# Sums of a weight matrix's quarters: made twice, or made once, stored to DRAM and loaded

## The chip, the cores and the metric

The kernel runs on one core of a Trainium2 chip. The metric is the device time of one execution in microseconds (us). The kernel before took 429.52 us, the median of three runs (427.53 to 430.59).

## What is computed

The reference mixes two branches of the same input by a learned gate, for x of shape (1, 2048, 512), 32 heads of width 16 and a hidden width of 1376. In short form:

```python
g = sigmoid((x * gate_w).sum(-1, keepdims=True))

# branch a: linear attention with a two-sided softmax feature map
q, k, v = split_heads(x @ wqkv)                     # 32 heads, 16 wide
pq, pk  = q @ w_phi, k @ w_phi                      # per head 16 x 16
phi_q   = concat(softmax(pq), softmax(-pq))         # 32 wide; phi_k likewise
kv, z   = phi_k^T v, sum_s phi_k
o       = (phi_q kv) / (phi_q z + 1e-6)
a       = merge_heads(o) @ wo

# branch b: dense, Mish, dense
b = mish(x @ w1 + b1) @ w2                          # w1: 512 x 1376

out = g * a + (1 - g) * b
```

All is fp32. The factor on w_phi's drawn values is 200.

## The kernel before

**Precision.** Every matrix product is made of fp32r pieces: an operand is split into a high part (an fp32r copy, made on ScalarE) and a low part (operand minus high part, subtracted on GpSimd or VectorE), and three products are added in PSUM: high by high, high by low, low by high.

**Stages.** Eight chunks "A0" to "A7" run over the sequence and build the key side: kv and z. Then four blocks "B0" to "B3" of 512 rows make the query side, the second dense layer ("down"), the output projection ("wo") and the mix. The first dense layer ("up", w1 by x) is made in two superblocks, "S0" for the blocks 0 and 1 and "S1" for the blocks 2 and 3.

**Pairs.** Ten of the eleven column tiles of w1 are taken as five pairs per superblock. A pair's part of w1 is a 2 x 2 matrix of quarters, and so is the superblock's x; the four results are made of seven quarter products instead of eight (a scheme of Strassen and Winograd), which needs sums of w1's quarters and of x's quarters. `pair_ops(p)` defines the steps of a pair. For pair 0 in S1 they are called `S1.wr_0` and so on:

- `wr`: load the quarters into the tile w1r, on SP's queue.
- `wa`, `wb`: split the quarters that enter the products unsummed, into w1d and w1o (high parts on ScalarE, low parts on GpSimd).
- `ws` (function `su`, L687 to L690): four VectorE instructions that make the sums in place in w1r.
- `wc` (function `hi2`): one ScalarE copy, the high part of all the sums, into w1sh.
- `wd` (function `lo2`, L700): one GpSimd subtraction, the low part, into w1sl.
- `p1` to `p7`: the seven products on TensorE; `p5`, `p6`, `p3` and `p7` use w1sh and w1sl.
- `c1`, `c5`, `c6` (copies out of PSUM on ScalarE), `a2`, `a3`, `a7` (additions on VectorE, L740, L743, L746), `mA0` to `mB1` (Mish on ScalarE), `sB0`, `sB1` (stores of block 1's or 3's results "ab" to DRAM, L762).

The quarters of w1 are the same in both superblocks, and so are their sums; x's are not. In pair 0 of S1, w1sh and w1sl are the two halves of one tile w1e.

**Order.** A string, RUN, names every step of the program in the order in which it is to be issued. Each instruction is pinned, so every engine runs its own instructions in that order, and so does each DMA queue. Nearly all DMAs are issued from SyncE's queue ("SP"): a DMA that waits there, for a buffer or for its data, holds up those behind it. Buffers come from pools by tag: six tiles of 1024 columns "m4" (w1d, w1o, w1sh, w1sl, woh, wol among them), three of tag "tx" (w1r, raw, xr), and others.

**Around the pairs.** SP's queue carries, beside w1: the exponentials of a block's query side, transposed on VectorE (L969), stored as "ed" (L971) and read back as eight pieces "eT" (L992; the step `B2.mv0` reads eight); the query projections, stored as pqd and read back as "pq" (L950); the stored results "ab", read back as "actb" (L811); the key sums z, transposed on VectorE and sent as "zd" (L859) and read back, spread over the partitions, as "zb" (L863); VectorE multiplies E by zb at L954. The output projection's weights come as "raw" (L578).

Helper lines: every matmul is recorded at L118, every ScalarE activation at L138.

Of the kernel before, what the change touches and what calls it, by code (L numbers as in the profile page):

```python
# [8 lines left out]
F32 = mybir.dt.float32  # L9
# [5 lines left out]
P = 128  # L15
# [91 lines left out]
def tile_gated_mix(ctx: ExitStack, tc: tile.TileContext, xT, wv, wkT, wqT, bd, w1a, w1b, b1, w2a, w2b, wo, out):  # L107
# [6 lines left out]
    pin = tc.keep_in_program_order  # L114
    V, G_, A_, Sy = nc.vector, nc.gpsimd, nc.scalar, nc.sync
# [4 lines left out]
    def T(shape, dt, tag, bufs, name):  # L120
        nm[0] += 1
        return sp.tile(shape, dt, name=f"{name}_{nm[0]}", tag=tag, bufs=bufs)

    def k8(name, tag, dt=F32R):
        return T([P, 2048], dt, tag, {"x": 7, "eT": 2, "E": 2, "w2": 5}[tag], name)

    def k4(name, tag, dt=F32):
        return T([P, 1024], dt, tag, {"tx": 3, "m4": 6, "z": 1}[tag], name)
# [8 lines left out]
    def act(out_, in_, fn=AF.Copy, **k):  # L137
        return pin(A_.activation(out_, in_, fn, **k))  # L138

    def kt(t, f):  # L140
        return t[:, : KT * f].rearrange("p (k f) -> p k f", f=f)
# [4 lines left out]
    def f32(ap):  # L146
        return ap.bitcast(F32)
# [445 lines left out]
    def w1_dram(f):  # L593
        d, f, n = (w1a, f, NFA) if f < NFA else (w1b, f - NFA, NFB)
        return d.rearrange("p (k n f) -> p k n f", k=KT, n=n)[:, :, f : min(f + 2, n), :]

    def s_ops(q):
        key = ("S", q)
        bs = 2 * q, 2 * q + 1
# [49 lines left out]
        def pair_ops(p):  # L649
            fs = W2G[p]  # L650
            i0, i1 = 1 + 2 * p, 2 + 2 * p
            W, ps, v = {}, {}, {}
# [29 lines left out]
                pin(G_.tensor_sub(o[1], r[:, 2:, P:], f32(o[0])))  # L682

            def su():
                r = kt(W["r"], 256)
                a11, a21, a22, a12 = r[:, :2, :P], r[:, :2, P:], r[:, 2:, :P], r[:, 2:, P:]
                pin(V.tensor_add(a22, a22, a21))  # L687
                pin(V.tensor_add(a21, a21, a11))
                pin(V.scalar_tensor_tensor(a11, a11, -1.0, a22, op0=ALU.mult, op1=ALU.subtract))
                pin(V.tensor_sub(a12, a12, a11))  # L690

            def hi2():
                if q and not p:
                    W["8"] = k8("w1e", "eT")
                W["sh"] = W["8"][:, :1024] if "8" in W else k4("w1sh", "m4", F32R)
                act(W["sh"], W["r"])

            def lo2():
                W["sl"] = W["8"][:, 1024:] if "8" in W else k4("w1sl", "m4", F32R)
                pin(G_.tensor_sub(W["sl"], W["r"], f32(W["sh"])))  # L700

            def dv(k0):
                return [a[:, k0 : k0 + 2, :] for a in halves2(W["d"])]
# [61 lines left out]
            for name, fn in (("wr", ld), ("wa", hi1), ("wb", lo1), ("ws", su), ("wc", hi2), ("wd", lo2), ("p1", p1), ("p2", p2), ("p3", p3), ("p4", p4),  # L765
                             ("p5", p5), ("p6", p6), ("p7", p7), ("a2", a2), ("a3", a3), ("a7", a7),
                             ("c1", lambda: copy("A0", "a")), ("c6", lambda: copy("B0", "a")), ("c5", lambda: copy("B1", "b"))):
                at(key, f"{name}_{n}", fn)
# [5 lines left out]
        for p in range(NFB):  # L774
            pair_ops(p)

        for m in range(2):
            b, W = bs[m], {}
# [300 lines left out]
    for q in range(NB // 2):  # L1079
        wo_ops(q)  # L1080
        s_ops(q)
# [153 lines left out]
```

## Time and profile before

| | |
|---|---|
| median of three runs | 429.52 us (427.53 to 430.59) |
| the profiled execution | 432.84 us; span 431.1 us, mean granted clock 0.996 |
| TensorE busy (weight loads apart) | 422.3 us, 98% |
| VectorE | 369.3 us, 86% |
| GpSimd | 263.6 us, 61% |
| ScalarE | 253.6 us, 59% |
| DMA | 74.06 MB, mean 172 GB/s |

The profile records one execution. PE is TensorE's matmuls, PEld its weight loads, DVE VectorE, ACT ScalarE, POOL GpSimd; SPq is SyncE's DMA queue. Busy times are sums over the span. A row of a timeline gives start, length, engine, line, operation, output and input, and in brackets the idle time before it and what released it; a row of a group gives busy time, mean nanoseconds of one, and idle time before; a row of a DMA group gives the count, the size of one and the median us from issue to landing. The span runs from the first to the last record, and the time of the execution contains 1.7 us beside it.

### The profile page before, as it was taken

Reading aid. Unit: us, or ns where it says so; the run is one execution under the profiler, and the core shown is the slowest. Engines: PE = TensorE matmul, PEld = TensorE weight load, DVE = VectorE, ACT = ScalarE, POOL = GpSimd, SP = SyncE. Lnnn points to the kernel's source line nnn. Section 1 sums busy time; section 2 is a strip of 40 time slices with the busy share of each in tenths; the row PEclk is TensorE's granted clock in tenths of the full one; section 3 lists DMA queues with packets and bytes.
Section 4 is the critical chain, followed back from the end, with each engine's and each line's share of the span. In section 5 each row is a group of like instructions: output and inputs, shape, how many; then the busy total and the mean of one; then the engine's idle time right before and its main releaser. Section 6 shows DMA issues by size and latency. Waiting matters only on the chain. (4 is left out here: it accounts for less than half of the span.)

```text
span 431.1 us, 7558 instructions
## 1 busy us (share of the span) xinstructions
PE 422.3 (98%) x2772; PEld 340.2 (79%) x2772; DVE 369.3 (86%) x519; ACT 253.6 (59%) x373; POOL 263.6 (61%) x186
## 2 busy tenths in 40 slices
PE   8999999999998999899999999999999999999996
PEld 7888888888886877688878687788788887877875
DVE  3899789998998999998999998799989699999512
ACT  3574463646254899768679813467978467851131
POOL 2298868799674966635666494977455627541220
PEclk9999999999999999989999999999999999999999
DMA  7900597675988344433888477833533725555532
GB/s 260 366 34 28 164 273 182 140 179 126 209 171 214 108 134 123 160 109 122 235 249 281 165 239 237 281 91 122 177 119 143 232 73 188 179 199 168 197 121 75
DMA packets 52670, 74.06 MB, mean 172 GB/s; under 512 B 8085, under 2 KB 32149, under 8 KB 52633
## 3 DMA queue, kind: packets, MB, share of 16 engines
q1 hardware_dynamic: 50440, 66.36, 47.9%
q0 software_dynamic: 1904, 6.82, 9.5%
q8 instruction: 22, 0.36, 0.3%
q10 hardware_dynamic: 288, 0.39, 0.3%
q14 instruction: 16, 0.12, 0.1%
HBM read 43.53 MB, written 28.85 MB: 168 GB/s over the span
## 5 line engine op out<-in xcount | busy, mean ns | idle before, releaser
L118 PE MATMUL down<-w2g,h 128*128 128x512 f32 x316 | 98.5, 393 | 0.0
L118 PEld LDWEIGHTS down<-w2g,h 128*128 128x128 f32 x316 | 58.6, 188 | 14.8 <-issue 2.5
L118 PE MATMUL down<-w2g,l 128*128 128x512 f32 x158 | 61.8, 391 | 0.2 <-POOL l L824 0.2
L824 POOL TENSOR_TENSOR l<-act,h 128x512 fp32r<-128x512 f32 (+1 forms) x24 | 32.3, 1345 | 41.2 <-ACT h L138 16.7
L824 POOL TENSOR_TENSOR l<-actb,h 128x512 fp32r<-128x512 f32 x20 | 29.0, 1451 | 38.3 <-ACT h L138 20.7
L138 ACT ACTIVATE E<-E 128x1024 f32<-128x1024 f32 x32 | 33.4, 1057 | 16.5 <-DVE E L285 7.1
L118 PE MATMUL up<-x,w1sh 128*128 128x512 f32 x144 | 39.7, 397 | 2.2 <-DVE act L740 2.1
L118 PE MATMUL wo<-woh,ohl 128*128 128x512 f32 x128 | 40.9, 389 | 0.0
L118 PEld LDWEIGHTS down<-w2g,l 128*128 128x128 f32 x158 | 29.6, 188 | 7.5 <-POOL l L824 1.2
L118 PEld LDWEIGHTS up<-x,w1sh 128*128 128x128 f32 x144 | 26.7, 189 | 9.2 <-DVE act L740 2.5
L700 POOL TENSOR_TENSOR w1sl<-w1r,w1sh 128x1024 fp32r<-128x1024 f32 x9 | 22.2, 2467 | 18.0 <-ACT w1sh L138 17.4
L118 PE MATMUL proj<-tw,sx 128*128 128x512 f32 x126 | 31.5, 394 | 1.5 <-ACT qs L138 1.5
L628 POOL TENSOR_TENSOR x<-xr,x 128x1024 fp32r<-128x1024 f32 x10 | 26.7, 2666 | 3.6 <-ACT x L138 3.6
L118 PEld LDWEIGHTS proj<-tw,sx 128*128 128x128 f32 x126 | 23.3, 188 | 6.9 <-ACT qs L138 1.9
L138 ACT ACT_TABLE_LOAD x22 | 28.2, 1283 | 0.4
L118 PEld LDWEIGHTS wo<-woh,ohl 128*128 128x128 f32 x128 | 24.0, 188 | 5.0
L138 ACT ACTIVATE act<-act,b1s 128x512 f32<-128x512 f32 x30 | 21.4, 719 | 10.9 <-DVE act L740 4.1
L118 PE MATMUL up<-x,w1d 128*128 128x512 f32 x108 | 27.7, 398 | 0.0
L267 POOL TENSOR_TENSOR xl<-xraw,xh 128x512 fp32r<-128x512 f32 x14 | 18.3, 1370 | 15.3 <-ACT xh L138 15.0
L138 ACT ACTIVATE act<-up 128x512 f32<-128x512 f32 x30 | 17.6, 590 | 16.8 <-PE up L118 16.4
L138 ACT ACTIVATE h<-actb 128x512 fp32r<-128x512 f32 x20 | 12.4, 628 | 24.4 <-DMA actb<-ab 18.9
L118 PE MATMUL wo<-wol,ohl 128*128 128x512 f32 x64 | 24.9, 389 | 0.0
(173 smaller groups left out, 1086.4 us busy)
## 6 DMA issues: line engine op xcount, KB each, us to landing
ed<-E SPq DMA_DIRECT2D x16, 512.0 KB, 3.1
eT<-ed SPq DMA_DIRECT2D x64, 128.0 KB, 3.2
za<-E POOLq DMA_DIRECT2D x11, 512.0 KB, 6.8
xr<-in_xT_dram SPq DMA_DIRECT2D x20, 256.0 KB, 4.2
ab<-act SPq DMA_DIRECT2D x20, 256.0 KB, 2.9
actb<-ab SPq DMA_DIRECT2D x20, 256.0 KB, 3.3
pqd<-qs SPq DMA_DIRECT2D x16, 256.0 KB, 5.8
pq<-pqd SPq DMA_DIRECT2D x16, 256.0 KB, 3.6
```

The lines of the kernel that those rows point to most:

```text
L118: return pin(nc.tensor.matmul(*a, **k))
L138: return pin(A_.activation(out_, in_, fn, **k))
L267: pin(eng.tensor_sub(xs[c][1][j], kt(rawx[c], SC)[:, 2 * j : 2 * j + 2, :], f32(xs[c][0][j])))
L628: pin((V if n in LOV else G_).tensor_sub(X[n][:, 1024:], xr[n], f32(X[n][:, :1024])))
L700: pin(G_.tensor_sub(W["sl"], W["r"], f32(W["sh"])))
L824: pin(G_.tensor_sub(U[i]["l"][:n, :], U[i]["a"][:n, :], f32(U[i]["h"][:n, :])))
```

## The change

The first superblock still makes the sums, their high part and their low part, and now also stores both parts to DRAM tiles (`wsd[p]`, two of 512 KB for each pair). The second superblock no longer makes them: `su` returns at once, and `hi2` and `lo2` load the stored parts into the tiles that they filled before. The steps keep their places in RUN.

```diff
@@ -594,6 +594,8 @@
+    wsd = {}
+
     def s_ops(q):
...
             def su():
+                if q:
+                    return
                 r = kt(W["r"], 256)
                 a11, a21, a22, a12 = r[:, :2, :P], r[:, :2, P:], r[:, 2:, :P], r[:, 2:, P:]
                 pin(V.tensor_add(a22, a22, a21))
@@ -693,11 +697,20 @@
                 if q and not p:
                     W["8"] = k8("w1e", "eT")
                 W["sh"] = W["8"][:, :1024] if "8" in W else k4("w1sh", "m4", F32R)
+                if q:
+                    pin(Sy.dma_start(f32(W["sh"]), wsd[p][0]))
+                    return
                 act(W["sh"], W["r"])
+                wsd[p] = [tc.dram_tile([P, 1024], F32, name=f"ws{p}_{x}") for x in range(2)]
+                pin(Sy.dma_start(wsd[p][0], f32(W["sh"])))
 
             def lo2():
                 W["sl"] = W["8"][:, 1024:] if "8" in W else k4("w1sl", "m4", F32R)
+                if q:
+                    pin(Sy.dma_start(f32(W["sl"]), wsd[p][1]))
+                    return
                 pin(G_.tensor_sub(W["sl"], W["r"], f32(W["sh"])))
+                pin(Sy.dma_start(wsd[p][1], f32(W["sl"])))
```

In the second superblock 20 VectorE, 5 ScalarE and 5 GpSimd instructions go, and ten loads of 512 KB come on SP's queue; in the first, ten stores of 512 KB come on the same queue. TensorE's order is unchanged. Lines after the change are 4 to 13 higher: the transpose is L982, ed's store L984, eT's reads L1005, a7 L759, the new loads L701 and L710, the new stores L705 and L713.

SP's queue in the second superblock, around pair 3. The names are tiles with their buffer numbers; `w1r<-in_w1a_dram` is a load for the eleventh column tile. Before:

```order
L971 DMA ed_3559<-E_3014 128x1024
L992 DMA eT_3561<-ed_3514 32x4x256 x4
L992 DMA eT_3561<-ed_3559 32x4x256 x4
L782 DMA w1r_3596<-in_w1a_dram 128x4x128
L578 DMA raw_3651<-in_wo_dram 32x2x512 x4
L950 DMA pq_3719<-pqd 128x512
```

And now:

```order
L984 DMA ed_3563<-E_3034 128x1024
L1005 DMA eT_3565<-ed_3518 32x4x256 x4
L1005 DMA eT_3565<-ed_3563 32x4x256 x4
L701 DMA w1sh_3574<-ws_0_2097 128x1024
L710 DMA w1sl_3584<-ws_1_2098 128x1024
L795 DMA w1r_3596<-in_w1a_dram 128x4x128
L701 DMA w1sh_3602<-ws_0_2246 128x1024
L710 DMA w1sl_3604<-ws_1_2247 128x1024
L578 DMA raw_3651<-in_wo_dram 32x2x512 x4
```

The loads of pair 3's two parts stand behind all eight reads of eT, and pair 4's behind one more load.

VectorE at pair 3 of the second superblock. `mn` is a reduction of the query side, `act` a pair's result, `E` and `Sm` the exponentials and their sums. Before:

```order
L743 TENSOR_TENSOR act_3449<-up_3418,act_3449 128x512
L275 TENSOR_REDUCE mn_3492<-pq_3253 128x32
L687 TENSOR_TENSOR w1r_3358<-w1r_3358 128x2x128
L688 TENSOR_TENSOR w1r_3358<-w1r_3358 128x2x128
L689 SCALAR_TENSOR_TENSOR w1r_3358<-w1r_3358 128x2x128
L690 TENSOR_TENSOR w1r_3358<-w1r_3358 128x2x128
L746 SCALAR_TENSOR_TENSOR act_3425<-up_3312,act_3425 128x512
L302 TENSOR_TENSOR E_3014<-E_3014,Sm_3167 128x1024
L969 STREAM_TRANSPOSE E_3014<-E_3014 128x1024
L291 TENSOR_REDUCE Sm_3544<-E_3124 128x64
L302 TENSOR_TENSOR E_3014<-E_3014,Sm_3032 128x1024
L969 STREAM_TRANSPOSE E_3014<-E_3014 128x1024
```

And now:

```order
L756 TENSOR_TENSOR act_3457<-up_3426,act_3457 128x512
L275 TENSOR_REDUCE mn_3500<-pq_3265 128x32
L759 SCALAR_TENSOR_TENSOR act_3433<-up_3324,act_3433 128x512
L302 TENSOR_TENSOR E_3034<-E_3034,Sm_3183 128x1024
L982 STREAM_TRANSPOSE E_3034<-E_3034 128x1024
L291 TENSOR_REDUCE Sm_3548<-E_3140 128x64
L302 TENSOR_TENSOR E_3034<-E_3034,Sm_3052 128x1024
L982 STREAM_TRANSPOSE E_3034<-E_3034 128x1024
```

The four sums are gone, and the addition a7 (`act<-up,act`) follows the reduction directly.

SP's queue in the first superblock, where the stores of pairs 1 and 2 come. `ge_sb` is the gate, `ab` a stored result. Before:

```order
L928 DMA ge_sb<-gd 128x4x1
L762 DMA ab_1_1807<-act_1652 128x512
L859 DMA zd<-zr_1801 32x32
L863 DMA zb_1885<-zd 128x1024
L950 DMA pq_1887<-pqd 128x512
```

And now:

```order
L941 DMA ge_sb<-gd 128x4x1
L705 DMA ws_0_1856<-w1sh_1854 128x1024
L713 DMA ws_1_1857<-w1sl_1865 128x1024
L775 DMA ab_1_1811<-act_1656 128x512
L872 DMA zd<-zr_1805 32x32
L876 DMA zb_1893<-zd 128x1024
L963 DMA pq_1895<-pqd 128x512
L705 DMA ws_0_1903<-w1sh_1901 128x1024
```

Pair 1's two stores stand ahead of ab's, zd's and zb's transfers.

## The prediction

> **What bounds the kernel now.** I read the busy shares first, then the stretches where the changed steps stand, then the timeline of the engine that is full there.
>
> ```profile
> PE 422.3 (98%) x2772; PEld 340.2 (79%) x2772; DVE 369.3 (86%) x519; ACT 253.6 (59%) x373; POOL 263.6 (61%) x186
> ```
>
> TensorE is busy 422.3 of 431.1 us. Work taken from another engine is worth time only where TensorE waits for it. The windows of the trace (start:end, length, then busy time of PE, PEld, DVE, ACT, POOL, granted clock, DMA share, GB/s) give this by stage:
>
> ```profile
> 165.00:185.00 20.00, 17.66 (x72) 13.61 (x71) 19.77 (x24) 15.33 (x21) 12.02 (x9) 0.95 0.57 170
> 280.00:337.00 57.00, 56.87 (x251) 46.05 (x250) 53.01 (x74) 43.71 (x67) 36.15 (x24) 1.00 0.42 136
> 337.00:425.00 88.00, 88.00 (x497) 69.68 (x496) 64.16 (x96) 42.38 (x66) 33.80 (x22) 1.00 0.49 160
> ```
>
> From 280 to 425, where the second superblock's w1 pairs are used, TensorE is modelled as idle for 0.13 us of 145. It has no slack that could absorb a late operand. From 165 to 185, in the first superblock, VectorE is full (19.77 of 20) and TensorE waits for it.
>
> **What goes.** Five pairs lose four VectorE sums, one ScalarE copy and one GpSimd subtraction each, all in the second superblock.
>
> ```profile
> L687 DVE TENSOR_TENSOR w1r<-w1r 128x256 f32<-128x256 f32 x10 | 6.3, 630 | 0.0
> L138 ACT ACTIVATE w1sh<-w1r 128x1024 fp32r<-128x1024 f32 x9 | 9.5, 1051 | 1.5 <-DVE w1r L690 1.5
> L700 POOL TENSOR_TENSOR w1sl<-w1r,w1sh 128x1024 fp32r<-128x1024 f32 x9 | 22.2, 2467 | 18.0 <-ACT w1sh L138 17.4
> ```
>
> Four sums at 0.4 to 0.63 us make about 2 us a pair, so VectorE loses some 10 us, ScalarE 5 x 1.05 = 5.3, GpSimd 5 x 2.47 = 12.3. In the windows above this lies beside a full TensorE, so it is costed at its effect on TensorE's small gaps there. Two of them are tied to ScalarE:
>
> ```profile
> 301.19 1.23 PEld L118 LDWEIGHTS up<-x,w1e 128*128 128x128 f32 x6 [0.36 <-ACT gr L138]
> 307.53 0.76 PEld L118 LDWEIGHTS up<-x,w1sh 128*128 128x128 f32 x4 [0.55 <-ACT act L138]
> ```
>
> Term **B**: with 1.05-us copies gone ahead of them these 0.36 and 0.55 us shrink. Bounds 0 and -1.0; I take **-0.4**, since weight loads overlap matmuls and not all of it was the path.
>
> **What comes.** Ten stores (first superblock) and ten loads (second) of 512 KB, 10.5 MB on 74.06, all in SP's queue, which is in program order. So the question is where each load stands in that queue and when TensorE wants the tile. I read the positions off the changed order and the times off the trace:
>
> ```profile
> 280.50 1.37 SPq L606 DMA_DIRECT2D xr<-in_xT_dram  x2
> 288.18 0.61 PE L118 MATMUL up<-x,w1e 128*128 128x512 f32 x2
> 296.50 0.47 SPq L663 DMA_DIRECT2D w1r<-in_w1b_dram  x1
> 315.95 0.38 SPq L950 DMA_DIRECT2D pq<-pqd  x1
> 320.57 1.07 PE L118 MATMUL up<-x,w1sh 128*128 128x512 f32 x4
> ```
>
> Pair 0's loads can issue next to the first row and are wanted from 288.18, over 6 us later. Pair 1's follow 296.50 and are wanted behind the weight loads at 301.19, which end at 302.42: 5.4 us. Pair 2's take the place at 315.95 and are wanted at 320.57: 4.6 us. All cover the landing taken below (4.0), so 0; a landing of 7.6 would cost up to 3.0 at pair 2. Pair 4's follow pair 3's directly and are wanted a whole pair later: 0. Pair 3's load stands behind the eight reads of B2.mv0, which wait for the two ed stores, which wait for VectorE's transposes:
>
> ```profile
> 326.12 0.42 DVE L687 TENSOR_TENSOR w1r<-w1r 128x256 f32<-128x256 f32 x1
> 327.89 0.68 DVE L746 SCALAR_TENSOR_TENSOR act<-up,act 128x512 f32<-128x512 f32 x1
> 333.25 1.25 DVE L969 STREAM_TRANSPOSE E<-E 128x1024 f32<-128x1024 f32 x1
> 334.53 0.32 SPq L971 DMA_DIRECT2D ed<-E  x1
> 334.96 4.24 SPq L992 DMA_DIRECT2D eT<-ed  x8
> 339.29 0.58 SPq L782 DMA_DIRECT2D w1r<-in_w1a_dram  x1
> 336.89 1.07 PE L118 MATMUL up<-x,w1sh 128*128 128x512 f32 x4
> 331.34 1.05 ACT L138 ACTIVATE w1sh<-w1r 128x1024 fp32r<-128x1024 f32 x1
> ```
>
> Before, the high part was made on ScalarE at 331.34 to 332.39 and never saw SP's queue. Now it can issue only where L782 stands, at 339.29, less what the missing sums give back. They ran from 326.12 to 327.89; but the instruction behind them, L746, reads a PSUM bank that TensorE finishes here:
>
> ```profile
> 325.56 0.62 PE L118 MATMUL up<-x,w1sl 128*128 128x512 f32 x2
> ```
>
> They end at 326.18, so L746 can start at about 326.27 instead of 327.89: the chain to the queue comes 1.62 us earlier and the load issues at 339.29 - 1.62 = 337.67, or 0.78 us after TensorE wants the tile. Then it must land. No row shows this load; the nearest ones are:
>
> ```profile
> ed<-E SPq DMA_DIRECT2D x16, 512.0 KB, 3.1
> w1r<-in_w1a_dram SPq DMA_DIRECT2D x8, 256.0 KB, 3.9
> xraw<-in_xT_dram SPq DMA_DIRECT2D x7, 512.0 KB, 7.6
> za<-E SPq DMA_DIRECT2D x2, 512.0 KB, 2.6
> 334.00:339.00 5.00, 5.00 (x24) 4.14 (x23) 4.84 (x8) 2.28 (x3) 3.69 (x2) 1.00 0.76 256
> ```
>
> The same size takes 2.6 to 7.6 us. The DMA engines are 0.76 busy just there (the 1 MB of eT), so I take 4.0, nearest to the loads of the same tag. Term **C** = 0.78 + 4.0 = **+4.8** (bounds 0.78 + 2.6 = 3.4 and 0.78 + 7.6 = 8.4). Behind the waiting matmul stands all of TensorE's queue, full until 425, so the stall goes to the end of the program in full.
>
> **The clock after a stall.** The profile has one longer wait of TensorE with a lower clock behind it, and one shorter wait without:
>
> ```profile
> 140.18 1.66 PE L118 MATMUL proj<-tw,sx 128*128 128x512 f32 x6 [1.52 <-ACT qs L138]
> 182.49 1.62 PE L118 MATMUL up<-x,w1sh 128*128 128x512 f32 x4 [2.08 <-DVE act L740]
> 184.76 2.33 PE L118 MATMUL up<-x,w1d 128*128 128x512 f32 x6
> 186.93 1.09 PE L118 MATMUL up<-x,w1sh 128*128 128x512 f32 x4
> 335.53 1.52 PE L118 MATMUL up<-x,w1o 128*128 128x512 f32 x6
> ```
>
> At full speed six such matmuls start 336.89 - 335.53 = 1.36 us apart from the next, 0.227 each. The twelve from 182.49 to 186.93 took 4.44 instead of 2.72, so 1.72 us went to a reduced clock (0.95 over that window). Term **D**: after a stall of 4.8 the same, **+1.7**; bounds 0 (as after the 1.52-us wait) and 2. The Trainium skill, "TensorE: Matmul & The Clock Gate", section "Part 1: The HAM clock gate (the "warmup" mystery)", says that the clock is halved after a whole idle window of about 3.4 us; the trace disagrees on the length, since 2.08 us sufficed here. By that rule D would hold only for stalls over 3.4 us, which leaves it in the sum as C is forecast, and drops it at C's lower bound.
>
> **The stores.** In the first superblock pair 1's two stores stand in SP's queue ahead of zd and zb, and the second waits for GpSimd's low part:
>
> ```profile
> 162.84 2.88 POOL L700 TENSOR_TENSOR w1sl<-w1r,w1sh 128x1024 fp32r<-128x1024 f32 x1 [4.57 <-ACT w1sh L138]
> 162.91 0.32 SPq L859 DMA_DIRECT2D zd<-zr  x1
> 164.25 0.32 SPq L863 DMA_DIRECT2D zb<-zd  x1
> 169.39 2.50 POOL L700 TENSOR_TENSOR w1sl<-w1r,w1sh 128x1024 fp32r<-128x1024 f32 x1 [0.31 <-PE up L118]
> 169.55 3.43 DVE L954 TENSOR_TENSOR T<-E,zb 128x1024 f32<-128x1024 f32 x1
> ```
>
> GpSimd ends at 165.72; zd then goes at some 166.4 instead of 162.91, and zb, 1.34 behind it, at 167.8 instead of 164.25. VectorE's first read of zb starts at 169.55, so zb landed in at most 5.3 us; 3.5 later that read starts up to 3.3 us late. But it is stretched now (3.43, ending when GpSimd's 169.39 + 2.50 is over and some 1.1 us more); started late it should be short, about 1.5, and end at most about 1.4 to 2.3 late. VectorE is full from there to TensorE's wait at 182.49, so what is late arrives. Term **A**: bounds 0 and 2.3; I take **+0.7**, half of the 1.4, since the landing may have had a us in hand. The other eight stores stand ahead of loads whose readers are behind other work of their engines; costed 0, covered by that work, and without the cover each would be worth a queue wait like A's.
>
> **Sum**: C 4.8 + D 1.7 + A 0.7 + B -0.4 = +6.8. Against the profiled execution (432.84 us whole, 431.1 span) this gives 439.6. That execution lies 3.3 above the median of the three runs, 429.52; on the median it gives **436.3**. Lower bounds together: 3.4 + 0 + 0 - 1.0 = +2.4; upper: 8.4 + 2 + 2.3 - 0 = +12.7.
>
> **Rivals.**
>
> R1, short and unthrottled. The load lands as ed does, 3.1, and the clock holds: 0.78 + 3.1 + 0.7 - 0.4 = +4.2, 433.7. For it: the median of 16 transfers of this size; against it: the 0.76 share, and that a 2.08-us wait was enough for the clock.
>
> R2, crowding. The 2 MB of pairs 3 and 4 share the DMA engines with eT and wo, and a landing takes xraw's 7.6: 8.4 + 1.7 + 0.7 - 0.4 = +10.4, 439.9. For it: 7.6 is the median of seven 512-KB loads. Against: those went out in the program's densest stretch.
>
> R3, not slower. Relief of VectorE and GpSimd brings the transposes forward far enough. One blocking is visible:
>
> ```profile
> 316.51 2.41 POOL L700 TENSOR_TENSOR w1sl<-w1r,w1sh 128x1024 fp32r<-128x1024 f32 x1
> 317.95 1.03 DVE L962 SCALAR_TENSOR_TENSOR den<-Dn 128x32 f32<-128x32 f32 x1
> ```
>
> L962 does 32 elements a lane and takes 1.03 us while GpSimd's subtraction runs to 318.92; it would end sooner without it. The Trainium skill, "SBUF — State Buffer", section "SBUF: two separate sides", says VectorE and GpSimd share a port pair that one instruction locks until it ends; this row agrees. It decides from the point where SP reaches the load by 336.89 - 4.0 = 332.9, 4.8 us earlier than my 337.67. Against it: L746 is held by TensorE's 326.18, and from there 1.22-us multiplies and 1.25-us transposes remain. Then C and D are 0: 0.7 - 0.4 = +0.3, or -1.0 with the bounds of A and B: 428.5 to 429.8.
>
> That the change does not do what it says is out: the changed order has 20 VectorE, 5 ScalarE and 5 GpSimd rows fewer and 20 DMAs more.
>
> **How the numbers follow.** A measurement of this kernel tells about 1% (4.3 us) from no change. Forecast 0.60 (slower), R1 0.13 (433.7, just within 1%), R2 0.13 (slower), R3 0.14 (within 1% 0.09; 0.05 if relief is worth more than any gap that I see). So slower 0.73, within 1% 0.22, faster 0.05. The forecast's own range is 433.8 to 439. For 8 in 10 I take 430.0 to 441.0, which leaves out R3 and the crowded end of R2.
>
> **What would show it.** Right: a wait of TensorE of 4 to 6 us in front of an up matmul on w1sh shortly after 337, released by a DMA into w1sh on line 701; a granted clock under 1 in the 5 us behind; the load issued directly behind L1005's eT reads; zb issued about 3.5 us later than 164.25, and the wait at 182.49 near 2.8. Wrong: TensorE without a gap there; a landing of the 512-KB loads far from 4; a new gap at pair 2 (near 320) or at pairs 0 and 1; or time lost in the first superblock of more than 2 us.

## The result

The changed kernel takes 442.99 us, the median of four runs (440.69 to 445.02), against 428.52 (425.81 to 430.59, four runs) for the kernel before: a ratio of 1.031, 95% interval 1.025 to 1.037. It is slower by 3.1%, where 1.6% was forecast (436.3), and it lies above the stated range (430 to 441). Measured again later on one chip, beside three of its variants, it was 1.037 (1.031 to 1.043). Here and below a ratio is an estimate from the fast runs of both kernels alone, so it differs a little from the quotient of two medians. The direction and the main place were right; the two terms that make most of the cost, the late load and the stores, were too small.

The page of the changed kernel, its busy shares and what its DMAs moved:

```profile
PE 426.1 (96%) x2772; PEld 341.3 (77%) x2772; DVE 357.4 (81%) x499; ACT 248.7 (56%) x368; POOL 252.1 (57%) x181
DMA packets 55550, 84.56 MB, mean 191 GB/s; under 512 B 8404, under 2 KB 32468, under 8 KB 55512
```

VectorE lost 12 us of work, GpSimd 11.5, ScalarE 5; TensorE's share fell from 98 to 96% of a longer span. The view of what TensorE waits for (total us, times, longest) names two new waits:

```profile
PE up L118 <- DMA w1sh<-ws: 6.9, 1, 6.9
PE up L118 <- DVE act L759: 1.9, 1, 1.9
```

The first is pair 3 of the second superblock. SP's queue and TensorE around it:

```profile
336.42 0.32 SPq L984 DMA_DIRECT2D ed<-E  x1
336.83 4.26 SPq L1005 DMA_DIRECT2D eT<-ed  x8
341.19 0.38 SPq L701 DMA_DIRECT2D w1sh<-ws  x1
...
338.71 1.52 PE L118 MATMUL up<-x,w1o 128*128 128x512 f32 x6
347.15 2.04 PE L118 MATMUL up<-x,w1sh 128*128 128x512 f32 x4 [6.92 <-DMA w1sh<-ws]
...
351.80 0.40 PE L118 MATMUL down<-w2g,l 128*128 128x512 f32 x1
```

Six matmuls that start at 338.71 at full speed are followed after 1.36 us, so TensorE wanted w1sh at 340.07. The load issued at 341.19, right behind the eight eT reads, and TensorE went on at 347.15, 5.96 us after the issue. This group starts 10.26 us later than before (336.89). Some matmuls on, the row at 351.80 stood here before:

```profile
339.38 0.39 PE L118 MATMUL down<-w2g,l 128*128 128x512 f32 x1
```

It is 12.42 us later, 2.2 us more than the group on w1sh, and these went to a reduced clock. The windows (start:end, length, busy PE, PEld, DVE, ACT, POOL, granted clock, DMA share, GB/s) show it, and the traffic ahead of it:

```profile
335.00:347.00 12.00, 5.23 (x24) 3.99 (x22) 5.51 (x9) 2.38 (x3) 3.33 (x3) 0.91 0.82 267
347.00:353.00 6.00, 5.85 (x17) 4.65 (x18) 0.00 (x0) 1.81 (x3) 0.00 (x0) 0.62 0.88 269
```

The second new wait belongs to the first superblock. SP, VectorE and TensorE there:

```profile
164.18 0.33 SPq L705 DMA_DIRECT2D ws<-w1sh  x1
167.13 0.32 SPq L713 DMA_DIRECT2D ws<-w1sl  x1
168.01 0.67 SPq L872 DMA_DIRECT2D zd<-zr  x1
170.59 0.32 SPq L876 DMA_DIRECT2D zb<-zd  x1
...
175.95 1.22 DVE L967 TENSOR_TENSOR T<-E,zb 128x1024 f32<-128x1024 f32 x1 [4.95 <-DMA zb<-zd]
...
179.55 1.85 PE L118 MATMUL up<-x,w1d 128*128 128x512 f32 x6 [1.89 <-DVE act L759]
```

VectorE, full at this place before, stands for 4.95 us until zb has landed, and TensorE then waits for an addition behind it.

This second wait stands in place of another one. The trace before has a stall of its own here, 2.08 us at 182.49 with a reduced clock behind it, and the changed trace has none in front of that matmul. e4, an experiment below, runs the first superblock as the kernel before does. The window of this stretch, in the changed kernel and then in e4:

```profile
165.00:185.00 20.00, 17.64 (x69) 13.48 (x68) 14.86 (x17) 14.12 (x19) 12.69 (x8) 0.91 0.69 252
165.00:185.00 20.00, 20.00 (x90) 16.57 (x89) 19.77 (x27) 17.93 (x26) 14.86 (x9) 1.00 0.66 198
```

The trace before had TensorE busy for 17.66 us of it at a clock of 0.95, hardly more than the changed one; e4 has it busy throughout. So the profiled execution of the kernel before had lost time at the very place where the stores delay zb. TensorE's order is the same in all these kernels, so its matmuls can be compared one by one: from 165 to 190 the changed trace loses 0.4 us against the trace before, and 5.2 us against e4's. Each of these is one execution.

### The profile page after: what moved, and what is told of

Same layout as the page of the kernel before. It is cut to its first block, busy times and chain, and to the rows that moved or that the text cites. A ratio compares the mean times of both kernels' runs of the same rounds, so it can differ in the third digit from the quotient of the medians.

```text
span 443.3 us, 7555 instructions
## 1 busy us (share of the span) xinstructions
PE 426.1 (96%) x2772; PEld 341.3 (77%) x2772; DVE 357.4 (81%) x499; ACT 248.7 (56%) x368; POOL 252.1 (57%) x181
## 4 chain that ended last, share of the span: by engine, by line
PE 69%; DVE 13%; DMA 10%; issue 3%; SPq 2%; ACT 1%; POOL 1%; DVEq 0%; POOLq 0%; ACTq 0%
PE proj L118 26%; PE up L118 17%; PE down L118 15%; PE wo L118 6%; DMA ed<-E 2%; DMA raw<-in_w2a_dram 2%; DVE Sm L291 2%; PE kvp L118 1%; DVE E L302 1%; DVE E L982 1%; DMA w1sh<-ws 1%; SPq L1005 1%; DMA zb<-zd 1%; PE num L118 1%; PE warm L118 1%
## 5 line engine op out<-in xcount | busy, mean ns | idle before, releaser
L118 PE MATMUL down<-w2g,h 128*128 128x512 f32 x316 | 100.3, 399 | 0.0
L837 POOL TENSOR_TENSOR l<-act,h 128x512 fp32r<-128x512 f32 (+1 forms) x24 | 35.3, 1473 | 64.7 <-PE down L118 25.2
L118 PEld LDWEIGHTS down<-w2g,h 128*128 128x128 f32 x316 | 60.0, 192 | 15.4 <-issue 2.1
L967 DVE TENSOR_TENSOR T<-E,zb 128x1024 f32<-128x1024 f32 x16 | 23.3, 1464 | 6.2 <-DMA zb<-zd 4.9
L118 PEld LDWEIGHTS up<-x,w1d 128*128 128x128 f32 x108 | 20.0, 188 | 7.0 <-DVE act L759 2.9
```

The source lines that it names most:

```text
L118: return pin(nc.tensor.matmul(*a, **k))
L837: pin(G_.tensor_sub(U[i]["l"][:n, :], U[i]["a"][:n, :], f32(U[i]["h"][:n, :])))
L967: pin(V.tensor_mul(d["T"], d["E"], B["zb"]))
```

## The experiments

Three theories stood against each other. **Q**: the place of the new transfers in SP's queue makes the cost, pair 3's late load above all. **T**: the traffic itself, 10.5 MB, makes it wherever the transfers stand. **R**: the relief of VectorE is worth something that the cost hides. Ratios are to the kernel before on the same chip, with their 95% intervals.

**Pair 3's loads early** (e1). The two steps move in RUN:

```diff
- ... B2.es0 B2.tr0 S1.sB1_2 ... B2.mv0 S1.wc_3 ... S1.wd_3 ...
+ ... B2.es0 B2.tr0 S1.wc_3 S1.wd_3 S1.sB1_2 ... B2.mv0 ...
```

> The changed kernel with pair 3's two loads of the second superblock moved ahead on SP's queue, directly behind the first of the two ed stores (tr0) instead of behind the eight eT reads. Theory Q (the load's place in SP's order makes the stall): the load issues near 333 instead of 341, has 7 us until TensorE wants it at 340, the 6.9-us stall and the about 2.2 us of reduced clock behind it go; about 9 us less than the changed kernel, near 434. Theory T (the added traffic itself makes loads slow wherever they stand): a landing of 6 to 10 us leaves a stall of 0 to 3 us and the clock loss; 437 to 441.

435.77 us, ratio 1.0115 (1.0056 to 1.0173). SP and TensorE:

```profile
332.16 1.04 SPq L701 DMA_DIRECT2D w1sh<-ws  x1
...
337.91 1.52 PE L118 MATMUL up<-x,w1o 128*128 128x512 f32 x6
339.27 1.07 PE L118 MATMUL up<-x,w1sh 128*128 128x512 f32 x4
```

TensorE has no wait at pair 3 and no reduced clock behind it. This supports theory Q: the same bytes, issued 7 us ahead of use, cost next to nothing there (TensorE loses 0.3 us in the next 3). About 1.2% stayed.

**Pair 4 made again** (e2). For pair 4, the condition `if q:` becomes `if q and p not in (4,):` in `su`, `hi2` and `lo2`, with a guard that keeps the second superblock from storing, so the 1 MB behind pair 3's loads is gone.

> The changed kernel with pair 4 of the second superblock made again as before (sums, copy, subtraction), so that its two 512-KB loads do not follow pair 3's. Theory Q with crowding from behind: pair 3's load lands in about 4 us instead of 5.9, since 1 MB less shares the DMA engines; the stall falls from 6.9 to about 5, the whole by 2 to 441. Rival (only what stands ahead counts, or the landing of a DRAM tile of this size is always near 6): stall within 0.5 of 6.9, time within 1 us of 443.

444.63 us, ratio 1.0331 (1.0266 to 1.0396).

```profile
340.48 0.38 SPq L701 DMA_DIRECT2D w1sh<-ws  x1
...
345.65 2.05 PE L118 MATMUL up<-x,w1sh 128*128 128x512 f32 x4 [6.10 <-DMA w1sh<-ws]
```

The landing fell from 5.96 to 5.17 us and the wait from 6.92 to 6.10: less than the 2 us of crowding theory, and more than the 0.5 of its rival. The time did not fall. The four traces that keep both pairs' loads late (the change, f1, and e11 and f3 below) have 5.96 to 6.19 us from issue to matmul, so the 0.8 us is more than their scatter, though it is one trace: what follows the load on the queue seems to lengthen its landing, but not by much.

**Stores only** (e3). The same condition and guard for all five pairs: the second superblock makes everything again, and the stores of the first stay.

> First superblock stores the ten tiles, the second makes everything again as before and loads nothing. My prediction's term A: +0.7 on before (429). Reading of the changed trace: TensorE is already 3 us late when the second superblock's pair 3 comes, so the stores alone cost about +3 (431.5), split between a wait near 141, the stretch 167 to 186 and small gaps up to 285. If the stores are free, the 3 us belong to the loads.

435.32 us, ratio 1.0123 (1.0054 to 1.0192): the stores alone cost some 5 us, all of what the first experiment left, though nobody reads what they store.

```profile
172.07 1.23 DVE L970 TENSOR_TENSOR T<-E,zb 128x1024 f32<-128x1024 f32 x1 [4.99 <-DMA zb<-zd]
...
175.67 1.66 PE L118 MATMUL up<-x,w1d 128*128 128x512 f32 x6 [1.71 <-DVE act L762]
181.76 1.19 PE L118 MATMUL up<-x,w1sh 128*128 128x512 f32 x4 [1.71 <-DVE act L756]
```

The wait for zb is there in full without any load: it comes from the stores.

**Sums left out** (e4). In the kernel before, `su` returns at once if q. The second superblock then works with unsummed quarters; the copy and the subtraction stay.

> The kernel before without the four VectorE sums of the second superblock (left out; the copy and the subtraction stay, so the products there use unsummed quarters), no stores, no loads. It prices the relief of VectorE by itself. My term B and rival R3: TensorE is full there, so between 0 and -1 us (428). If the relief were worth much (theory R: freed VectorE brings transposes and reads forward), -2 or more.

430.59 us, ratio 1.0021 (0.9979 to 1.0063). Taking 10 us of work from VectorE in the second superblock gains nothing that can be measured. Theory R falls for VectorE; the relief of ScalarE and GpSimd was never taken alone, and is contained in e9 below, which shows no gain either.

**Loads early, pair 1's stores late** (e5), and **stores only, pair 1's late** (e6). Pair 1's two stores become a step of their own behind zb:

```diff
- ... A7.zs A7.zl B1.lq3 S0.ws_2 ...
+ ... A7.zs A7.zl S0.wt_1 B1.lq3 S0.ws_2 ...
```

> Pair 3's loads moved ahead as in the first experiment, and pair 1's two stores of the first superblock issued behind zd and zb instead of ahead of them. Theory Z (most of what the stores cost is zb arriving late): VectorE's 5-us wait for zb goes back to nothing, and with it about 3 of the remaining 5 us over before: 1.004 +- 0.004 of before. Theory T (the stores cost by their traffic, in many small waits): stays at 1.01.

> First superblock stores, second superblock makes everything again and loads nothing; pair 1's stores issued behind zd and zb. Against the stores-only run (1.0123 of before): theory Z 1.003 to 1.006, the rest being the small waits between 195 and 310; theory T no change, 1.011 to 1.013.

e5: 432.45 us, ratio 1.0058 (1.0016 to 1.0100). e6: 433.48 us, ratio 1.0066 (1.0022 to 1.0111). In e5:

```profile
164.31 0.32 SPq L881 DMA_DIRECT2D zd<-zr  x1
165.66 0.33 SPq L885 DMA_DIRECT2D zb<-zd  x1
166.08 0.38 SPq L718 DMA_DIRECT2D ws<-w1sh  x1
...
170.95 1.21 DVE L976 TENSOR_TENSOR T<-E,zb 128x1024 f32<-128x1024 f32 x1
```

VectorE's wait is gone. Against e1 and e3 the ratios fall by 0.6% each, which is half of the stores' cost; the intervals overlap, and e1 and e3 ran on another chip, so the size of this half is not settled by these. The traces agree on the place: between 165 and 190 TensorE gains 2.4 to 4.8 us on the trace before in the seven traces with pair 1's stores late, and in the eight with them in front it is between 0.5 us worse and 0.9 better. e5 and e6 differ by the loads (present, absent) and come out the same: no cost of the ten loads, with pair 3's early, can be seen.

**Loads ahead of the eT reads** (e7) and **on ScalarE's queue** (e8), one run each:

```diff
- ... B2.tr1 B2.mv0 S1.wc_3 ...          (e7)
+ ... B2.tr1 S1.wc_3 S1.wd_3 B2.mv0 ...
- pin(Sy.dma_start(f32(W["sh"]), wsd[p][0]))                               (e8, and the same for "sl")
+ pin((nc.scalar if p == 3 else Sy).dma_start(f32(W["sh"]), wsd[p][0]))
```

e8 also moves the step `S1.wd_3` directly behind `S1.wc_3` in RUN, so that both loads go out together.

> The changed kernel with pair 3's two loads directly ahead of the eight eT reads (behind both ed stores) instead of directly behind them. They issue 4.4 us earlier in the program's frame (near 336.8 where TensorE wants the tile at 340). If the 5.9-us landing came from what stands ahead in the queue (1 MB of eT), it falls to about 3.3 and TensorE waits under 0.5 us; if the transfers issued behind it share the DMA engines as well, or a landing of this size is near 6 there anyway, 5 to 6 and a wait of 2 to 3 us.

> The changed kernel with pair 3's two loads issued from ScalarE's queue at the same place of the program, so that SP's order does not hold them. ScalarE gets there at about 333.8 (7 us ahead of SP). Theory Q: issued near 334, landed by 339, no wait of TensorE before w1sh of pair 3; the time near that of the first experiment (435.8), about 8 us under the changed kernel. If the place in SP's queue were not the cause, the wait stays above 3 us.

e7 took 437.24 us in its one run:

```profile
335.74 0.38 SPq L701 DMA_DIRECT2D w1sh<-ws  x1
336.97 5.62 SPq L1005 DMA_DIRECT2D eT<-ed  x8
...
340.62 1.16 PE L118 MATMUL up<-x,w1sh 128*128 128x512 f32 x4 [1.48 <-DMA w1sh<-ws]
342.32 0.73 PE L118 MATMUL up<-x,w1sl 128*128 128x512 f32 x2 [0.54 <-DMA w1sl<-ws]
```

With no eT read ahead of it the load still took 4.88 us to the matmul, between the two expectations (3.3, or 5 to 6). Late or early, with eT's reads ahead or not, a load of this size took 4.9 to 6.2 us at this place; in e1, issued at 332.16, it landed after 5.5. e8 took 436.48 us in its one run:

```profile
333.74 0.34 ACTq L701 DMA_DIRECT2D w1sh<-ws  x1
...
340.64 1.07 PE L118 MATMUL up<-x,w1sh 128*128 128x512 f32 x4
```

Issued from another queue at the same place of the program, the load is in time and the wait gone. It was SP's order.

**Pair 4's stores late too** (e9), and **pair 4 neither stored nor loaded** (e10), both on top of e5. For e9, `S0.wt_4` comes behind `S0.ldo1`, the second load of wo.

> As the fifth experiment (pair 3's loads early, pair 1's stores late), and pair 4's two stores of the first superblock behind the loads of wo instead of ahead of an ed store, eight eT reads and those loads. Theory P (what is left of the cost, 0.6%, is again stores standing in front on SP's queue, here pair 4's): the small waits from 231 to 283 go, 1.000 to 1.003 of before. Theory T (the traffic itself): as the fifth, 1.004 to 1.008.

> As the fifth experiment, with pair 4 made in both superblocks and neither stored nor loaded (8.4 MB more than before instead of 10.5). Theory P: like the ninth, 1.000 to 1.003. Theory T: a fifth of the remaining cost goes, 1.005. If the waits from 231 to 283 stay with no store of pair 4 anywhere, neither its place nor its bytes made them.

e9: 431.93 us, ratio 0.9995 (0.9960 to 1.0030). e10: 430.71 us, ratio 0.9961 (0.9921 to 1.0000). All ten stores and all ten loads are in e9, and it is no different from the kernel before. Theory T falls as the cause of the 3%: 84.6 MB instead of 74.1 cost at most 0.3% by e9's interval, 0.7% by that of f4 below. The queue where pair 4's stores stood, in e5 and then in e9:

```profile
201.34 0.34 SPq L706 DMA_DIRECT2D ws<-w1sh  x1
...
204.48 0.46 SPq L715 DMA_DIRECT2D ws<-w1sl  x1
...
206.83 5.65 SPq L1014 DMA_DIRECT2D eT<-ed  x8
```

```profile
203.74 4.17 SPq L1014 DMA_DIRECT2D eT<-ed  x8
```

With the stores ahead, SP needed 5.65 us to issue the eight eT reads in e5, without them 4.17 in e9. Over all traces the two groups overlap: 4.17 to 5.65 us in the ten with these stores ahead, 3.68 to 5.38 in the seven without. Nor did TensorE's small waits go in e9, as was expected: between 190 and 310 they sum to 1.6 us there, with one of 1.01 for eT that is new, to 2.2 in e5, and to 0.2 in e10. Against the trace before, TensorE loses 1.2 to 3.1 us in this stretch in the ten traces with pair 4's stores in front, 1.4 to 4.1 in the four with them behind, and nothing in e10, which does not store pair 4. So it is not shown that the place of pair 4's stores matters; as far as the traces go it is the storing itself, at 1 to 4 us. In the medians e9 and e10 are 0.3% apart, within the intervals, and e5 ran on another chip than both.

**The change with the stores late** (e11): RUN as in the change for pair 3, stores as in e9.

> The changed kernel with the stores of pairs 1 and 4 moved behind zb and behind wo's loads as in the ninth experiment, and pair 3's loads left where the change put them. If the two parts add (stores about 1.15%, pair 3's late load about 1.95%), the ratio to before is 1.016 to 1.022, with the wait of 6 to 7 us before w1sh of pair 3 and about 2 us of reduced clock in the trace. If they do not add (the stores' delay had been hiding some of the load's, or the reverse), under 1.013 or over 1.025.

435.90 us, ratio 1.0110 (1.0059 to 1.0161), though its trace has the same 6.91-us wait at pair 3. The two parts would have left 1.019, and 1.016 to 1.022 was expected, so this one missed.

**Two by two on one chip** (f1 to f4): the change, e1's kernel, e11's and e9's, measured in turn.

> The change itself again, as one corner of a two by two on one chip (pair 3's loads late or early; the stores of pairs 1 and 4 in front or behind). Additive: 1.031 +- 0.003 of before. If its first measurement was high by chance: 1.02 to 1.025.

> Second corner: pair 3's loads early, stores as in the change. As measured before, 1.0115 +- 0.003; so pair 3's late load is worth 1.9% with the stores in front.

> Third corner: loads as in the change, stores behind. Additive: 1.031 less 1.2%, that is 1.019. Interaction (the late load costs less when the stores are out of the way, as the eleventh experiment suggests): 1.011, under 1.014.

> Fourth corner: loads early, stores behind. 1.000 +- 0.003. The interaction is the first corner less the second less the third plus the fourth: 0 if the two parts add, 0.8% if the eleventh experiment is right.

| ratio to before | stores in front | stores behind |
|---|---|---|
| pair 3's loads late | 1.0370 (1.0308 to 1.0431), 445.33 us | 1.0210 (1.0139 to 1.0281), 438.91 us |
| pair 3's loads early | 1.0144 (1.0081 to 1.0207), 436.25 us | 1.0014 (0.9960 to 1.0067), 431.79 us |

The late load costs 2.3% with the stores in front and 2.0% with them behind; the stores' place costs 1.6% and 1.3%. The interaction is 0.3%, well inside the intervals of some 0.6% on each ratio, so the two parts add as far as this can tell. Together they are the whole of the change's cost, and the corner without both is no different from before. The stores' place stands here for both groups together, pair 1's and pair 4's. f3 is e11's kernel, 1.0210 here and 1.0110 there: two series of one kernel can lie 1% apart, so the steps of 0.6% above should not be leaned on.

## Why the prediction was too low

**Bound and place: right in the second superblock.** TensorE absorbed nothing there, the relief was worth nothing (B: -0.4 forecast, nothing measurable found), and the stall stood where it was put, behind the eT reads at pair 3, with no wait for a load at pairs 0, 1, 2 and 4 in the changed trace. In e11's trace the load of pair 1 cost 0.96 us.

**C, pair 3's load: right mechanism, landing too short.** In the changed kernel TensorE is 3.18 us later than before when it comes to pair 3 (340.07 for 336.89). Taking this off, ed's second store moved from 334.53 to 336.42 - 3.18 = 333.24, 1.29 us earlier where 1.62 was worked out. The load issued 341.19 - 340.07 = 1.12 us after the want, where 0.78 was forecast. The landing was 5.96 instead of 4.0. So C was 7.1, not 4.8, within its bounds of 3.4 and 8.4. What failed is the choice of the row: the 4.0 leaned on w1r's 3.9, taken as loads of the same tag. They are 256 KB, half the size, and by the list of pools w1r is of tag tx and w1sh of m4. The changed page shows the new stores and loads apart:

```profile
ws<-w1sh SPq DMA_DIRECT2D x5, 512.0 KB, 2.6
ws<-w1sl SPq DMA_DIRECT2D x5, 512.0 KB, 3.2
w1sh<-ws SPq DMA_DIRECT2D x4, 512.0 KB, 5.2
w1sl<-ws SPq DMA_DIRECT2D x4, 512.0 KB, 7.1
```

Tiles of one size took 2.6 to 3.2 us to DRAM and 5.2 to 7.1 from it, in stretches that were busy to different degrees; these are medians, and a single store took up to 5.9. The page before had 512-KB loads at 6.0 (wv, not used in the forecast) and 7.6 (x); those were the nearest rows, and I left the second to a rival, as the program's densest stretch.

**D, the clock: nearly right in size.** 2.2 us, where 1.7 was forecast with an upper bound of 2. C and D together were 6.5 in the forecast and 9.3 in the trace; the two by two gives 7 to 9 us in the medians.

**A, the stores: wrong, 0.7 for 4 to 6 us** (e3 and f2, by medians and by ratios), about twice its upper bound of 2.3. Four steps failed. First, zb's lateness: I moved it by the wait for GpSimd and the issue alone, 3.5 us. Pair 1's second store went at 167.13 where I had 165.72, so 1.4 us of the times here are a shift that the program already had; without it zb issued 170.59 - 164.25 - 1.4 = 4.9 us later. zd had to land before zb could go, and behind the stores that took 170.59 - 168.01 = 2.6 instead of 1.34; zb's own landing then reached 175.95, 5.4 us after the issue, where VectorE waited 4.95. Second, the halving: I took half of 1.4 because the landing "may have had a us in hand". VectorE's 4.95 us show that nothing near enough was in hand. Third, the way to TensorE. I let the lateness arrive at the wait of 182.49, as 2.8 instead of 2.08. It arrived earlier, as the 1.89 us at 179.55, with a clock of 0.76 from 179 to 186, and the other wait went. The forecast was worked out on an execution that already lost 2.08 and 1.72 us here, which e4's trace does not, so next to it a late zb looked cheap. Fourth, the other eight stores at nothing. "Readers behind other work of their engines" was never worked out for them, and pair 4's cost TensorE 1 to 4 us in the traces, wherever they stood, if e10's one trace is the measure; by which step they do so stays open.

C, D and A as found, 7.1, 2.2 and 4 to 6, make 13 to 15 us; the two medians differ by 14.5.

**Rivals.** R2 gave the landing nearest to what came (7.6, against 5.96), R1 and R3 did not occur. No rival had the stores as the place of its cost, and even the upper bounds together, 12.7 us, came to 442.2.

## What to carry to other kernels

A transfer added to a queue that runs in program order can be paid for by everything behind it. Go through each new DMA, not only the largest, and ask what stands behind it on the queue and when that is wanted; in a chain of two dependent transfers (zd, zb) both are delayed. Here the bytes cost little or nothing (0.3 to 0.7% at most) and the work saved earned nothing that could be measured; where the steps stood in the order cost 3%, and with pair 3's loads and two pairs' stores moved the time went back to that of before. There was no gain left to collect: TensorE, busy for 98% of the span, set the end, and the relieved engines did not. And ask of the one execution that a forecast is built on whether it had a bad moment just where the change acts.

## What the runs showed of the hardware

**The clock after a wait does not go by the length of the wait alone.** In e8, a wait of 1.88 us at 140.68 is followed by a granted clock of 0.72; in e1, one of 2.00 us is not. The row of each wait and its window:

```profile
140.68 1.86 PE L118 MATMUL proj<-tw,sx 128*128 128x512 f32 x6 [1.88 <-ACT qs L138]
140.00:146.00 6.00, 5.32 (x16) 4.22 (x17) 3.64 (x6) 5.37 (x9) 6.00 (x4) 0.72 0.40 149
```

```profile
178.80 1.66 PE L118 MATMUL up<-x,w1d 128*128 128x512 f32 x6 [2.00 <-DVE act L759]
175.00:189.00 14.00, 10.29 (x44) 7.87 (x44) 13.77 (x20) 8.35 (x12) 8.39 (x6) 1.00 0.82 284
```

The waits of 6.1 us (e2) and 6.9 (the change) were followed by clocks of 0.64 and 0.62. The Trainium skill, "TensorE: Matmul & The Clock Gate", section "Part 1: The HAM clock gate (the "warmup" mystery)", describes a window of about 3.4 us that runs freely, and a clock that is halved after at least one idle window. A window that runs freely fits a dependence on where the wait falls; the 3.4 us of idleness does not fit, as 1.88 sufficed. For a forecast this means, as an estimate from the 2.08 us of the trace before and the 1.72 lost behind it, that 2 us of wait may cost 2 or 4.

**Issuing reads takes longer shortly behind large loads, on whichever queue these were issued.** At pair 3 the eight eT reads took 4.20 to 4.27 us to issue in the nine traces without the new loads ahead of them, 5.62 in e7 with two 512-KB loads directly ahead, and 7.37 to 7.90 in the seven traces with the two loads issued some 4 us before them. The first row is e9's, the second e8's, whose loads went out on ScalarE's queue:

```profile
330.22 7.65 SPq L1014 DMA_DIRECT2D eT<-ed  x8
337.40 7.37 SPq L1005 DMA_DIRECT2D eT<-ed  x8
```

So it is not only what stands on SP's own queue; the cause stays open. In e9 it cost little: TensorE did not wait for eT there.
